# Attention ahead of a mixture of experts: input sets loaded in thirds, weight conversion moved to later steps with four word buffers

## The chip, the cores and the metric

One core of a Trainium2 chip runs the whole program. The metric is the device time of one execution in microseconds (us), taken as the median over runs. The engines are named as the profile names them: PE is TensorE's matmul, PEld its weight load, DVE is VectorE, ACT is ScalarE, POOL is GpSimd and SP is SyncE, which here issues transfers.

## The reference

Three layers follow each other. The first is attention with a sigmoid in place of the softmax, for 4 batches of 12 heads with 448 positions of 64 elements. Its output, laid out as 1792 tokens of 768, goes through a gate that gives each of 8 experts 224 tokens, and then through a feed-forward layer.

```python
scores = scale * np.matmul(q, k.transpose(0, 1, 3, 2)) - np.log(S)
attn = 1.0 / (1.0 + np.exp(-scores))
x = np.matmul(attn, v)
...
logits = x @ w_gate
...
h = np.maximum(x[mask] @ w1[e], 0.0)
out[mask] = h @ w2[e]
...
h = x @ w_in
g = np.maximum(h, 0.0) + alpha * np.minimum(h, 0.0)
return g @ w_out
```

The last layer's weights w_in and w_out arrive as 64-bit floating-point numbers, two 32-bit words each.

## The kernel before, in words

**The attention stage.** The heads are taken in 12 sets of four (three sets a batch). A set's q, k and v lie side by side in one tile `qkv` of 128 partitions, 1344 KB: q in its first third, k in its second, v in its last. The pool that holds it has three buffers. A set takes seven steps (`STEPS_OF`, L338): three for its first pair of heads, one for what is left of both pairs, three for the second pair. So there are 84 steps, numbered i. In each, `scores(i)` makes eight matmuls (L350) and one sigmoid on ACT (L353), and two steps later `values` makes eight matmuls with the result (L373). At the end of a pair ACT copies an accumulator out (L377, L381) and DVE adds the other (L379, L382).

**What is put between the steps.** After each batch, `turns` transposes the batch's output and stores its rows to DRAM (L315 on PE, L318 on ACT, L320 on SP), one of four turns a step, from the third step of the next batch's first set. Then `after_batch` computes the gate and compares the tokens' gate values with those of all tokens before them (L197 and L199 on DVE, L206 on PE), a little in every step and more in the later batches.

**The conversion of the last layer's weights.** `narrow` (L386) is a generator that turns the 64-bit words of w_in (16 parts) and of the first 13 blocks of w_out into 32-bit floating-point numbers, 29 parts in all. A part is fetched into a `words` tile by a transfer that POOL issues (L398, L400). ACT takes the absolute value of the upper words (L405, every second part; DVE does the others, L419) into `ct` and scales the lower words into `cl` (L427). DVE clamps, shifts and joins (L423, L425, L429), POOL adds `ct` and `cl` (L440), and the parts of w_out are stored to DRAM by a transfer of POOL's (L410). When part i has been added, the fetch of part i + 3 is issued, since there are three `words` buffers. The generator stops after each piece of its work, 102 times in all; `aside(i)`, called twice in each step, adds PACE to an account and takes one piece for each whole unit.

**The order of the work** is that of the program: each engine, and each engine's queue of transfers, takes its instructions in the order in which the Python code writes them, and waits only for data and for free buffers. A transfer that stands at some step of the code is thus issued as soon as its engine gets there. The main loop (L496 on) writes, for each step: scores, loads of later sets, `aside`, values, one piece of the work after a batch, `aside`.

**The loads.** Set 0 is loaded in five pieces before the loop: q and k of its first pair, v, q and k of its second pair (L105 to L109, all on SP). Set 1 is loaded in one transfer by ACT's queue after the first step's scores. Set n + 2 is loaded in one transfer on SP at the fourth step of set n, into the buffer of set n - 1.

```python
            if i == 0:
                load(1, eng=nc.scalar)
            n, at_step = divmod(i, len(STEPS_OF))
            if at_step == LATE + 1 and n + 2 < B * NQ:
                load(n + 2)
        aside(i)
```

Of the kernel before, what the change touches and what calls it, by code (L numbers as in the profile page):

```python
# [24 lines left out]
def attention_experts_ffn(  # L25
# [11 lines left out]
    nc = tc.nc  # L37
    B, NQ, P = qkv.shape[:3]
    N, DM = out.shape
# [38 lines left out]
    cv = att.enter_context(tc.tile_pool(name="cv", bufs=3))  # L78
# [7 lines left out]
    QV = 2 * S  # L86
    KC = S // P
    qkv_sb = {}

    def load(n, a=0, z=3 * QV, eng=nc.sync):  # L90
        if a == 0:
            qkv_sb[n] = ld.tile([P, 3 * QV], F32, name="qkv")
        eng.dma_start(qkv_sb[n][:, a:z], qkv[n // NQ, n % NQ, :, a:z])

    def q_of(n, r):
        return qkv_sb[n][:, r * S:(r + 1) * S]
# [4 lines left out]
    def v_of(n, c, h):  # L101
        o = 2 * QV + (c * 4 + h) * D
        return qkv_sb[n][:, o:o + D]

    load(0, 0, S)  # L105
    load(0, QV, QV + S)
    load(0, 2 * QV, 3 * QV)
    load(0, S, QV)
    load(0, QV + S, 2 * QV)  # L109

    warm = const.tile([1, 1], F32, name="warm")
    nc.vector.memset(warm, 0.0)
# [190 lines left out]
    def turns(b):  # L303


        x = xT[b]

        def turn(t0):
            w = min(P, S - t0)
            xt = aw.tile([P, DM], F32, name="xt", bufs=3)  # L310
            p = ps_s.tile([P, 2, 512], F32, name="psc")
            for i in range(HP):
                for s in range(w // D):
                    for z in range(2):
                        nc.tensor.matmul(p[halves[s], z, i * D:(i + 1) * D],  # L315
                                             x[halves[z], i, t0 + s * D:t0 + (s + 1) * D],
                                             ident[halves[z], halves[z]], start=True, stop=True)
            nc.scalar.copy(xt[:w].rearrange("p (i z d) -> p z i d", z=2, d=D),  # L318
                           p[:w, :, :HP * D].rearrange("p z (i d) -> p z i d", d=D))
            nc.sync.dma_start(x_dram[b * S + t0:b * S + t0 + w, :], xt[:w])  # L320

        return [lambda t0=t0: turn(t0) for t0 in range(0, S, P)]
# [7 lines left out]
    def keep_warm(ps, tag, n):  # L330
        p = ps.tile([P, 512], F32, name=tag)[:, :3 * P]
        for _ in range(n):
            nc.tensor.matmul(p, idle[:, :P], idle, start=True, stop=True)
# [6 lines left out]
    LATE = 2  # L340
    halves = [slice(0, D), slice(D, P)]

    def scores(i):
        n, r, c = steps[i]
        p = ps_s.tile([P, 2, 512], F32, name="psc")
        for s in range(2):
            for z in range(2):
                a = c * P + z * D if r is not None else KC * P
                w = r if r is not None else z
                nc.tensor.matmul(p[halves[z], s, :S], k_of(n, w, a, a + D)[halves[s]], q_of(n, w)[halves[s]],  # L350
                                 start=True, stop=True)
        AT[i] = aw.tile([P, 2, S], F32, name="at", bufs=LATE + 2)
        nc.scalar.activation(AT[i], p[:, :, :S], AF.Sigmoid, bias=bias, scale=1.0 / math.sqrt(D))  # L353

    def values(i):
        n, r, c = steps[i]
        b, m = divmod(n, NQ)
        if (r, c) == (0, 0):
            if m == 0:
                xT[b] = aw.tile([P, HP, S], F32, name="xT")  # L360
            PV[0, 1] = ps_v.tile([P, 512], F32, name="pav")
            PV[0, 0] = ps_v.tile([P, 512], F32, name="pav")
        if r is None:
            PV[1, 1] = ps_v.tile([P, 512], F32, name="pav")
        if (r, c) == (1, 0):
            PV[1, 0] = ps_v.tile([P, 512], F32, name="pav")
        a = AT.pop(i)
        for z in range(2):
            w = r if r is not None else z
            first = (w, z) == (1, 1) and r is None or (w, z) != (1, 1) and c == 0  # L370
            last = (w, z) == (0, 0) and r is None or (w, z) != (0, 0) and c == KC - 1
            for s in range(2):
                nc.tensor.matmul(PV[w, z][halves[s], :S], v_of(n, c, 2 * w + s if r is not None else s)[halves[z]],  # L373
                                 a[halves[z], s, :], start=first, stop=last)
        x = xT[b]
        if (r, c) == (0, KC - 1):
            nc.scalar.copy(x[:, 2 * m, :], PV[0, 1][:, :S])  # L377
        elif r is None:
            nc.vector.tensor_tensor(x[:, 2 * m, :], x[:, 2 * m, :], PV[0, 0][:, :S], op=OP.add)  # L379
        elif (r, c) == (1, KC - 1):  # L380
            nc.scalar.copy(x[:, 2 * m + 1, :], PV[1, 1][:, :S])  # L381
            nc.vector.tensor_tensor(x[:, 2 * m + 1, :], x[:, 2 * m + 1, :], PV[1, 0][:, :S], op=OP.add)  # L382
# [87 lines left out]
    FA = 13  # L470
    if wide:
        back = narrow([(True, f, 0) for f in range(NF)] + [(False, f, 0) for f in range(FA)],
                      cv, DM, ("words", 3), ("ct", 4), ("cl", 3))
    else:
        back = iter(())
        for f in range(NF):
            nc.gpsimd.dma_start(w_in_sb[:, :, f * P:(f + 1) * P], w_in[f].rearrange("p (c f) -> p c f", f=P))
# [3 lines left out]

    def aside(i):

        if i > 2:
            owed[0] += PACE
            while owed[0] >= 1:
                next(back, None)
                owed[0] -= 1

    nc.sync.dma_start(wg[:, :, :E], w_gate.rearrange("(c p) e -> p c e", p=P))  # L490
    nc.sync.dma_start(al, alpha.rearrange("(c p) -> p c", p=P))
    PACE = 0.64
    keep_warm(ps_m, "pm", 14)
    NS = len(steps)
    BS = NQ * len(STEPS_OF)
    for i in range(NS + LATE):  # L496
        if i < NS:
            scores(i)
            if i == 0:
                load(1, eng=nc.scalar)  # L500
            n, at_step = divmod(i, len(STEPS_OF))
            if at_step == LATE + 1 and n + 2 < B * NQ:
                load(n + 2)
        aside(i)
        k = i - LATE
        if k == NS - 1:
            final = after_batch(B - 1)
            final.pop(0)()
        if k >= 0:
            values(k)  # L510
        for turns_left in (rows_todo, todo):
            if turns_left:
                turns_left.pop(0)()
                break
        aside(i)
        if k >= 0 and k % BS == BS - 1:
            b = k // BS
            todo += after_batch(b) if b + 1 < B else final
            (rows_todo if b + 2 < B else rows_end).extend(turns(b))
# [777 lines left out]
```

## Time and profile before

| | |
|---|---|
| median of 3 runs | 1025.6 us (1024.71 to 1025.71) |
| the profiled execution | 1016.1 us |
| its span, first to last instruction | 1014.3 us |
| mean granted clock of TensorE | 0.977 |
| busy in the span: PE, DVE, ACT, POOL | 965.7, 659.2, 524.4, 223.0 us |
| attention stage | from 5.9 to about 187 us of the span |

The profiled execution is a single one and was 9.5 us shorter than the median of the timed runs. Times in the rows are microseconds from the start of its span. Busy time counts an engine's instructions, not its waits. In a row of a timeline, the bracket at the end gives the idle time of the engine ahead of the instruction and what ended it. A granted clock of 1.00 is the full clock of TensorE, 2.4 GHz, and 0.50 is half of it.

### The profile page before, as it was taken

How to read it: one execution, taken by the hardware profiler on the slowest of the kernel's cores; microseconds unless marked ns; L12 is line 12 of the kernel's file. 1: busy time of each engine (PE TensorE's matmuls, PEld its weight loads, DVE VectorE, ACT ScalarE, POOL GpSimd, SP SyncE). 2: the span in 40 equal slices, each digit the busy share in tenths (PEclk: the TensorE clock that was granted, in tenths of full speed). 3: DMA queues.
4: the chain of work that ended last, by engine and by line, in shares of the span. 5: the costliest groups of instructions: out<-in, count | busy, mean ns of one | idle time of the engine just before them, and what ended most of it. 6: DMA issues, size and time to landing. Idle time of an engine off the chain costs nothing.

```text
span 1014.3 us, 17190 instructions
## 1 busy us (share of the span) xinstructions
PE 965.7 (95%) x6729; PEld 792.4 (78%) x6729; DVE 659.2 (65%) x1258; ACT 524.4 (52%) x875; POOL 223.0 (22%) x300
## 2 busy tenths in 40 slices
PE   6999989869899999999999999999999999999995
PEld 2444433568898888899988899999899999999994
DVE  1868769797777685477777645876543477744342
ACT  3987867511364334366643344675443466644441
POOL 1545354221750001711000060300120111000001
PEclk8999999969899999999999999999999999999998
DMA  7776794465661220357303131871231157311211
GB/s 258 262 289 237 274 323 165 177 215 158 191 190 40 63 95 32 84 178 256 125 32 109 47 113 39 272 232 35 94 91 61 45 181 254 119 47 47 63 32 55
DMA packets 38643, 141.44 MB, mean 139 GB/s; under 512 B 8931, under 2 KB 9523, under 8 KB 37155
## 3 DMA queue, kind: packets, MB, share of 16 engines
q1 hardware_dynamic: 23186, 71.02, 21.7%
q0 software_dynamic: 15232, 67.95, 20.3%
q8 instruction: 53, 0.87, 0.4%
q10 hardware_dynamic: 144, 1.38, 0.3%
q14 instruction: 28, 0.22, 0.1%
HBM read 122.86 MB, written 17.46 MB: 138 GB/s over the span
## 4 chain that ended last, share of the span: by engine, by line
PE 74%; DVE 9%; ACT 7%; DMA 5%; issue 3%; POOL 2%; SPq 0%; DVEq 0%; ACTq 0%; POOLq 0%
PE pa L1129 20%; PE pz L1109 19%; PE pa L1027 15%; PE psc L350 4%; PE pav L373 4%; ACT si L963 2%; PE pa L912 2%; PE pa L932 2%; DMA qkv<-in_qkv_dram 1%; PE pa L1109 1%; PE pc L206 1%; DVE t L1030 1%; DVE g L199 1%; PE psc L315 1%; POOL pk L740 1%
## 5 line engine op out<-in xcount | busy, mean ns | idle before, releaser
L1129 PE MATMUL pa<-gx,so 128*128 128x448 f32 x1152 | 252.4, 369 | 0.4 <-DVE so L1074 0.3
L1109 PE MATMUL pz<-y,si 128*128 128x448 f32 x1080 | 231.0, 367 | 1.2 <-ACT R L182 1.2
L1129 PEld LDWEIGHTS pa<-gx,so 128*128 128x128 f32 x1152 | 213.9, 188 | 21.2 <-issue 2.5
L1109 PEld LDWEIGHTS pz<-y,si 128*128 128x128 f32 x1080 | 202.0, 188 | 19.3 <-ACT R L182 1.7
L1112 ACT ACTIVATE gx<-pz 128x448 f32<-128x448 f32 x60 | 32.7, 546 | 250.1 <-PE pz L1109 250.1
L1114 DVE SCALAR_TENSOR_TENSOR gx<-gx,nalpha 128x448 f32<-128x448 f32 x64 | 43.8, 684 | 151.9 <-ACT gx L1113 151.8
L1067 POOL DMA_DIRECT2D wo<-wo_dram x64 | 35.7, 559 | 438.9 <-DVE so L1074 253.8
L1027 PE MATMUL pa<-y,si 128*128 128x448 f32 x336 | 111.9, 386 | 1.2 <-DVE y L990 1.2
L1027 PE MATMUL pa<-gx,si 128*128 128x448 f32 x336 | 107.8, 378 | 0.0
L350 PE MATMUL psc<-qkv 64*64 64x448 f32 x672 | 98.2, 565 | 8.4 <-DMA qkv<-in_qkv_dram 6.8
L373 PE MATMUL pav<-at,qkv 64*64 64x448 f32 x672 | 99.8, 552 | 5.9 <-ACT xT L381 5.1
L353 ACT ACTIVATE at<-psc,bias 128x896 f32<-128x896 f32 x84 | 84.2, 1009 | 40.8 <-PE psc L350 40.5
L968 DVE TENSOR_TENSOR so<-wm,si 128x768 fp32r<-128x768 f32 (+1 forms) x98 | 103.9, 1064 | 2.1 <-PE pa L1129 1.1
L963 ACT CAST si<-wm 128x768 fp32r<-128x768 f32 (+1 forms) x98 | 89.7, 920 | 0.9 <-DMA wm<-in_w_dram 0.9
L1027 PE MATMUL pa<-gx,so 128*128 128x224 f32 x336 | 83.1, 268 | 0.5
L1027 PE MATMUL pa<-y,so 128*128 128x224 f32 x336 | 81.9, 271 | 1.6 <-DVE so L968 1.6
L373 PEld LDWEIGHTS pav<-at,qkv 64*64 64x64 f32 x672 | 33.6, 137 | 46.5 <-issue 32.6
L1027 PEld LDWEIGHTS pa<-y,so 128*128 128x128 f32 x336 | 65.4, 195 | 4.9 <-DVE so L968 2.2
L1030 DVE TENSOR_TENSOR t<-pa,t 128x224 f32<-128x224 f32 x98 | 38.3, 391 | 45.4 <-ACT t L1029 45.2
L1027 PEld LDWEIGHTS pa<-y,si 128*128 128x128 f32 x336 | 62.5, 193 | 5.1 <-ACT si L963 1.4
L1027 PEld LDWEIGHTS pa<-gx,so 128*128 128x128 f32 x336 | 63.9, 190 | 3.2 <-DVE so L968 2.2
L1118 DVE TENSOR_TENSOR gx<-gx 128x448 fp32r<-128x448 f32 x64 | 40.1, 626 | 40.5 <-ACT gx L1117 40.5
(209 smaller groups left out, 1445.5 us busy)
## 6 DMA issues: line engine op xcount, KB each, us to landing
wm<-in_w_dram SPq DMA_DIRECT2D x64, 384.0 KB, 3.6
wm<-in_w_dram SPq DMA_DIRECT2D x48, 512.0 KB, 4.5
wo<-wo_dram POOLq DMA_DIRECT2D x64, 384.0 KB, 3.4
qkv<-in_qkv_dram SPq DMA_DIRECT2D x10, 1344.0 KB, 8.4
words<-in_w_in_dram POOLq DMA_DIRECT2D x16, 768.0 KB, 5.5
words<-in_w_out_dram POOLq DMA_DIRECT2D x13, 768.0 KB, 5.9
wo_dram<-ct POOLq DMA_DIRECT2D x13, 384.0 KB, 3.5
x_dram<-xt SPq DMA_DIRECT2D x12, 384.0 KB, 4.2
```

Of the source, the lines that this page charges most:

```text
L350: nc.tensor.matmul(p[halves[z], s, :S], k_of(n, w, a, a + D)[halves[s]], q_of(n, w)[halves[s]], start=True, stop=True)
L353: nc.scalar.activation(AT[i], p[:, :, :S], AF.Sigmoid, bias=bias, scale=1.0 / math.sqrt(D))
L373: nc.tensor.matmul(PV[w, z][halves[s], :S], v_of(n, c, 2 * w + s if r is not None else s)[halves[z]], a[halves[z], s, :], start=first, sto ...
L963: nc.scalar.copy(hi, w)
L968: nc.vector.tensor_tensor(lo, w, hi.bitcast(F32), op=OP.subtract)
L1027: nc.tensor.matmul(o, a[:, c, :], y, start=(c == 0 and s == 0), stop=(c == k - 1 and s == 1))
L1030: nc.vector.tensor_tensor(t, p[:, :CAP], t, op=OP.add)
L1067: nc.gpsimd.dma_start(RW[f], wo_dram[f * P:(f + 1) * P, :])
L1109: nc.tensor.matmul(z[:, :n], a[:, c, :], m[:, c, :n], start=(c == 0 and s == 0), stop=(c == HP - 1 and s == 2))
L1114: nc.vector.scalar_tensor_tensor(t, dn, nalpha[:, f:f + 1], up, op0=OP.mult, op1=OP.add)
L1118: nc.vector.tensor_tensor(gl, t, gh.bitcast(F32), op=OP.subtract)
L1129: nc.tensor.matmul(acc[d][:, :n], a[:, d * P:(d + 1) * P], m, start=(f == 0 and s == 0), stop=(f == NF - 1 and s == 2))
```

## The change

There are four edits.

- `load` uses SP alone, and set 1 is loaded right behind set 0's pieces, in one transfer, where it was issued by ACT after the first step's scores.
- Set n + 2 is loaded in three transfers, q, k and v, at steps 3, 4 and 5 of set n, where it was one transfer at step 3.
- The conversion has four `words` buffers and two `cl` buffers, where it had three of each. The fetch issued after part i is thus that of part i + 4.
- `aside` begins at step 9 and no longer at step 3, and its pace is 0.68 of a piece a call, where it was 0.64.

```diff
--- before.py
+++ after.py
@@ -87,10 +87,10 @@
     KC = S // P
     qkv_sb = {}
 
-    def load(n, a=0, z=3 * QV, eng=nc.sync):
+    def load(n, a=0, z=3 * QV):
         if a == 0:
             qkv_sb[n] = ld.tile([P, 3 * QV], F32, name="qkv")
-        eng.dma_start(qkv_sb[n][:, a:z], qkv[n // NQ, n % NQ, :, a:z])
+        nc.sync.dma_start(qkv_sb[n][:, a:z], qkv[n // NQ, n % NQ, :, a:z])
 
     def q_of(n, r):
         return qkv_sb[n][:, r * S:(r + 1) * S]
@@ -107,6 +107,7 @@
     load(0, 2 * QV, 3 * QV)
     load(0, S, QV)
     load(0, QV + S, 2 * QV)
+    load(1)
 
     warm = const.tile([1, 1], F32, name="warm")
     nc.vector.memset(warm, 0.0)
@@ -470,7 +471,7 @@
     FA = 13
     if wide:
         back = narrow([(True, f, 0) for f in range(NF)] + [(False, f, 0) for f in range(FA)],
-                      cv, DM, ("words", 3), ("ct", 4), ("cl", 3))
+                      cv, DM, ("words", 4), ("ct", 4), ("cl", 2))
     else:
         back = iter(())
         for f in range(NF):
@@ -481,7 +482,7 @@
 
     def aside(i):
 
-        if i > 2:
+        if i > 8:
             owed[0] += PACE
             while owed[0] >= 1:
                 next(back, None)
@@ -489,18 +490,18 @@
 
     nc.sync.dma_start(wg[:, :, :E], w_gate.rearrange("(c p) e -> p c e", p=P))
     nc.sync.dma_start(al, alpha.rearrange("(c p) -> p c", p=P))
-    PACE = 0.64
+    PACE = 0.68
     keep_warm(ps_m, "pm", 14)
     NS = len(steps)
     BS = NQ * len(STEPS_OF)
     for i in range(NS + LATE):
         if i < NS:
             scores(i)
-            if i == 0:
-                load(1, eng=nc.scalar)
             n, at_step = divmod(i, len(STEPS_OF))
-            if at_step == LATE + 1 and n + 2 < B * NQ:
-                load(n + 2)
+
+            if LATE < at_step <= LATE + 3 and n + 2 < B * NQ:
+                a = (at_step - LATE - 1) * QV
+                load(n + 2, a, a + QV)
         aside(i)
         k = i - LATE
         if k == NS - 1:
```

## Rows read from the trace of the kernel before

**Rows 1.** The page's 40 slices of the span (25.4 us each), tenths

```profile
PE   6999989869899999999999999999999999999995
PEclk8999999969899999999999999999999999999998
```

**Rows 2.** Windows, 24 to 187 us: length; PE, PEld, DVE, ACT, POOL busy; PEclk

```profile
24.00:187.00 163.00, 153.52 (x1905) 66.62 (x1900) 129.47 (x190) 128.78 (x158) 78.82 (x68) 0.98 0.70 247
```

**Rows 3.** The chain of waits, 1 to 32 us: start, us, what

```profile
2.62 15.05 DMA qkv<-in_qkv_dram
```

**Rows 4.** DMA issues, 2 to 6 us: KB of each, median us to landing

```profile
qkv<-in_qkv_dram SPq DMA_DIRECT2D x2, 224.0 KB, 15.0
```

**Rows 5.** Timeline of PE: start, us, instructions [idle before, releaser]

```profile
17.81 1.02 PE L350 MATMUL psc<-qkv 64*64 64x448 f32 x3 [6.76 <-DMA qkv<-in_qkv_dram]
...
96.12 0.59 PE L373 MATMUL pav<-at,qkv 64*64 64x448 f32 x2 [1.52 <-ACT xT L381]
...
143.42 0.97 PE L373 MATMUL pav<-at,qkv 64*64 64x448 f32 x4 [2.58 <-ACT xT L381]
```

**Rows 6.** DMA queues, 6 to 18 us: packets, MB, share of 16 engines

```profile
DMA packets 3645, 3.95 MB, mean 329 GB/s; under 512 B 2929, under 2 KB 3160, under 8 KB 3517
...
q0 software_dynamic: 378, 2.03, 41.8%
q10 hardware_dynamic: 144, 1.38, 27.1%
```

**Rows 7.** Windows, two stretches after a stop of PE

```profile
17.80:22.30 4.50, 4.49 (x25) 1.72 (x29) 0.00 (x0) 1.01 (x1) 0.00 (x0) 0.51 0.88 307
...
97.00:101.00 4.00, 4.00 (x74) 2.06 (x73) 3.90 (x5) 2.60 (x3) 2.52 (x2) 0.57 0.87 310
```

**Rows 8.** Timeline of ACT and of POOL around two late words

```profile
93.84 0.92 ACT L405 ACTIVATE ct<-words 128x768 f32<-128x768 f32 x1 [1.32 <-DMA words<-in_w_in_dram]
...
141.16 0.90 ACT L405 ACTIVATE ct<-words 128x768 f32<-128x768 f32 x1 [2.10 <-DMA words<-in_w_out_dram]
...
128.89 0.60 POOL L400 DMA_DIRECT2D words<-in_w_out_dram  x1
...
133.87 0.59 POOL L400 DMA_DIRECT2D words<-in_w_out_dram  x1
```

**Rows 9.** Timeline of PE, POOL and SP at the start

```profile
5.88 1.73 PE L350 MATMUL psc<-qkv 64*64 64x448 f32 x16
...
9.33 0.98 PE L373 MATMUL pav<-at,qkv 64*64 64x448 f32 x8 [0.36 <-DMA qkv<-in_qkv_dram]
...
1.80 1.83 POOL L398 DMA_DIRECT2D words<-in_w_in_dram  x3
...
4.64 12.97 SPq L93 DMA_DIRECT2D qkv<-in_qkv_dram  x1
```

**Rows 10.** Timeline of ACT at step 9 and of DVE at the stage's end

```profile
30.76 1.02 ACT L353 ACTIVATE at<-psc,bias 128x896 f32<-128x896 f32 x1
...
187.11 0.62 DVE L382 TENSOR_TENSOR xT<-xT,pav 128x448 f32<-128x448 f32 x1 [2.07 <-ACT xT L381]
```

**Rows 11.** The tile qkv: DMA issues (ns, first and last start), landing times

```profile
L93 SPq DMA_DIRECT2D qkv<-in_qkv_dram x15: 327/370/12970, 0.8 to 139.4; - x15
...
DMA to landing us min/median/max: 2.6/8.0/18.4
```

**Rows 12.** Waits of SP's queue, 0 to 187 us: total, times, longest

```profile
SPq L93 <- PE pav L373: 71.6, 7, 12.8
```

**Rows 13.** Timeline of POOL (add 26) and of ACT (Copy 28)

```profile
176.16 2.04 POOL L440 TENSOR_TENSOR ct<-ct,cl 128x768 int32<-128x768 int32 x1 [2.17 <-ACT at L353]
...
180.72 0.94 ACT L427 ACTIVATE cl<-words 128x768 int32<-128x768 uint32 x1
```

**Rows 14.** Windows, instructions on ct (DVE, ACT, POOL), then on cl (ACT, POOL)

```profile
23.00:187.00 164.00, 88.62 (x101) 13.98 (x15) 63.63 (x42) 0.98 0.69 245
...
23.00:187.00 164.00, 26.94 (x29) 55.70 (x29) 0.98 0.69 245
```

## The prediction

> **What bounds the kernel now.** I read the page's slices first. TensorE is at nine tenths or more almost everywhere; the slices that are not full, and those where its clock is low, lie in the first quarter, which is the attention stage [rows 1]. The whole change lies in that stage, so I read only it. A window over 24 to 187 us shows that no engine is full there: TensorE 153.5 of 163.0 us, VectorE 129.5, ScalarE 128.8, POOL 78.8 [rows 2]. The stage is a chain that goes round between PE, ACT and DVE, and a stop of one of them soon stops PE. Behind the stage follow routing and the experts, whose start hangs on its end; I let a gain here reach the end of the program in full.
>
> Next I looked for the stops of PE. There are three that a transfer causes.
> - The start. The chain of waits has one transfer of 15.05 us, from 2.62 us [rows 3]: the last two pieces of set 0 (q and k of the second pair) took 15.0 us to land [rows 4], and step 3's scores, which need them, went on only at 17.81, after 6.76 us in which PE was idle [rows 5]. From 6 to 18 us POOL's words (2.03 MB) and ACT's load of set 1 (1.38 MB) were moved beside what was left of set 0 on SP's queue [rows 6]. From 17.8 to 22.3 us PE ran at a granted 0.51, the lower of its two levels, 1.2 GHz [rows 7].
> - ACT's Abs of words at 93.84 waited 1.32 us for its transfer, and PE then stood idle 1.52 us; ACT's Abs at 141.16 waited 2.10 us, and PE stood idle 2.58 us [rows 5, 8]. After each, the granted clock was 0.57 over four microseconds, 97 to 101 [rows 7] and 145 to 149 alike.
>
> **The change part by part.**
> *Set 1 from SP at once.* The load leaves ACT's queue and stands on SP's behind set 0's five pieces. What competes with the last two pieces is then the words alone. Lower bound of the landing: together these pieces have the 448 KB of the piece before them (set 0's v), which PE could use at 9.33 us, 3.45 us after the first pair (5.88) [rows 9]; at that rate they are there at 9.33 + 3.45 = 12.8. Upper bound: 17.8, nothing gained. Between them: the window moved 3.95 MB in 12 us, 0.33 MB a us, so without ACT's 1.38 MB [rows 6] they land some 4 us sooner. I take 14.0, a gain of 3.8 us; words' fourth transfer is the reason not to take the lower end. PE's idle time shrinks from 6.8 to about 3 us, but the stops of 1.5 and 2.6 us below also brought the low clock [rows 5, 7], so I leave in one such stretch: 0.43 missing of 4 us is 1.7 us lost. Before, 0.49 missing of 4.5 us lost 2.2: 0.5 us gained (bounds 0 and 2.2). Set 1 itself follows on the same queue: 1.38 MB at 0.33 MB a us is 4.2 us, 18.2 or, beside the words, 20 us. Step 7 comes four steps after step 3, which from 17.81 to step 9's sigmoid at 30.76 took 2.2 us each [rows 5, 10]: at 22. The tiny gate and alpha loads stand behind it; nobody needs them before step 23. SP stood 12.97 us in the issue of set 2 behind them, from 4.64 [rows 9], and the longest landing, 18.4 us [rows 11], is set 2's, at 23; with 4.2 us of set 1 ahead of it, it is there at some 28, and step 14 comes five steps after step 9, not before 33. No cost.
>
> The Trainium skill speaks against this gain: "DMA: Bandwidth & Descriptors", section "Issuing engines are not separate DMA queues", says that transfers started by any engine run on the same 16 engines and interleave, and that another issuer saves only issue time. By it alone the sum would have 0 for the first wait. The same page's "Queues, rings and completion order" has each engine take turns between the queues' rings, by which SP gets every second turn and not every third. I go by [rows 4, 6].
>
> *Thirds at steps 3, 4, 5.* Twenty more issues on SP, at 0.37 us in the median [rows 11], 7.4 us; SP waits 71.6 us for PE to release a set [rows 12], so they are hidden. Nothing on SP waits for a step: where no row store stands between, the three thirds are issued one after the other as soon as the buffer is free, so the spreading is mostly in the packets. After each batch's end the thirds stand behind row stores, and the last is up to two steps later. Set n+2 is needed eleven steps after step 3, some 22 us, nine after step 5, some 18; the median landing is 8.0 us [rows 11]. Cost 0; without that cover a late set would stop PE as the words do, 3 to 4 us a time.
>
> *Four word buffers.* At the start POOL's program has nothing ahead of the first fetches that waits, so they go out at 1.80 us whatever step they stand at [rows 9]: now four. Later every fetch goes out one part earlier. The fetch that came late at 141.16 left at 133.87, and would leave where the one before it left, at 128.89 [rows 8]: 5.0 us for a wait of 2.10. The one at 93.84 was later by less, and gains a part's length too. The two stops cost 1.52 + 2.58 us idle and 0.43 x 4 = 1.7 us each at the low clock [rows 5, 7]: 7.5 us together. VectorE and ScalarE get time back in such a stop, so I take 6.0 (bounds 0 and 7.5). POOL's one more issue at the start, 1.83 us for three [rows 9], 0.6, falls before it has anything to convert.
>
> *Two "cl" buffers.* ScalarE's Copy of part i must now wait for POOL's add of part i-2, not i-3. Nearest in time are the last parts: Copy 28 starts at 180.72, add 26 ended at 176.16 + 2.04 = 178.20, 2.5 us before [rows 13]. Cost 0 at this margin; it is the rival below.
>
> *Begin at i > 8, pace 0.68.* (That is six steps later, not five.) The 102 yields took 80 steps at 1.28, and take 75 at 1.36, to step 83 and not 82. About 6 x 1.28 = 7.7 yields move from steps 3 to 8 into the rest. VectorE's operations of the conversion sum to 88.6 us, 0.87 a yield, ScalarE's two to 14.0 + 26.9 = 40.9, 0.40 a yield [rows 14]: 6.7 and 3.1 us move. Bounds 6.7 (VectorE full), 0 (hidden wholly) and, below nothing, -3.1, ScalarE's work gone from steps 3 to 8. Its share was 129.5 of 163.0 [rows 2], so I take 0.79 x 6.7 = 5.3. At the end the last VectorE operation comes a step later, into 2.07 us that VectorE waits before 187.11 [rows 10]: 0.
>
> *Sum:* -3.8 - 0.5 - 6.0 + 5.3 = -5.0 us. The profiled execution took 1016.1 us (its span 1014.3) and would take 1011.1; the median of the timed runs is 1025.6, 9.5 above it, and I take the same difference off that: **1020.6 us**. 0.2%, 2.05 us, is about what a measurement of this kernel can tell from none: 1023.5 to 1027.7 is "same".
>
> **The rivals.**
> - *The denser conversion is hidden.* For it: 20% of VectorE's and ScalarE's time is free [rows 2]. Then -10.3 us: 1015.3.
> - *The first wait stays:* the same transfers share the same engines, and words' fourth takes the place of set 1's beside the last pieces. Against: words' packets were beside all of set 0 already, and ACT's came on top. Without the 4.3 us: 1024.9. The rule on issuing engines in the Trainium skill's "DMA: Bandwidth & Descriptors", above, would have it so.
> - *The words come late again,* because the transfers and not the buffers are short: the denser pace asks 6% more. For it: the late one took 141.16 - 133.87 = 7.3 us from issue to use [rows 8], more than a part's 5.4 (29 parts in the 156 us from 30.76 to 187.11 [rows 10]). Against: the two late ones miss by 2.1 us or less and leave 5 us earlier. -4.3 + 5.3 = +1.0: 1026.6.
> - *Slower: ScalarE waits for POOL.* In the third and fourth batch VectorE carries the comparisons too, falls behind, POOL's add follows it, and the Copy with two buffers holds ScalarE, its sigmoids and PE. It decides once add i-2 ends later than Copy i's place, 2.5 us beyond what [rows 13] show, at two places or more. Each costs like the two stops, (1.52 + 2.58) / 2 + 1.7 = 3.75. With VectorE full: -4.3 - 6.0 + 6.7 + 2 x 3.75 = +3.9: 1029.5.
> - *It does not do what it says:* the first fetches and most thirds do not move with their steps. That is in the sum already.
>
> **How the numbers follow.** Forecast 0.48, hidden conversion 0.17, first wait 0.10, words late again 0.11, slower 0.14. The second goes to faster with the forecast: 0.65. The third and fourth are same: 0.21. Slower 0.14. The forecast's own range is 1016.0 to 1023.5. The range for eight in ten takes in the centres of the hidden conversion, the first wait and the late words, and leaves out the slower rival and the tail below: 1014.0 to 1027.0.
>
> **What would show it.** Step 3's scores should go on at about 14 us and not 17.8, and step 9's sigmoid come at 26 and not 30.76 [rows 10]; ScalarE's Abs should wait for no words, and the low clock at 97 and 145 should be gone; the stage should end near 182 where it ended at 187. VectorE's share over the stage should rise. Wrong: a ScalarE Copy with a wait for POOL's add; PE waiting for qkv beyond step 3; a words wait above 1 us; new stretches at 0.5 after 30 us.

## The result, and the profile after

The changed kernel took 1011.48 us (1009.40 to 1013.34, four runs), the kernel before beside it 1025.65 us (1024.71 to 1031.52, four runs): a ratio of 0.9849 [0.9805, 0.9894]. That is faster, as forecast, but the forecast was 1020.6 us and its range ended at 1014.0. The profiled executions are closer: 1009.74 us after (span 1007.7) against 1016.1 before (span 1014.3), 6.4 us less, where the sum of the steps was 5.0. The kernel before has short executions (1011 to 1022 us) and long ones (1023 to 1033 us), in a mix that changes with the occasion: its recorded runs were long, its profiled execution was short, and the ratios below leave out runs over 1.5% above a kernel's fastest.

The page after; its slices answer to [rows 1]. The first slice, with PE's first stop, has gone from 6 to 7 and its clock from 8 to 9, and the sixth, with the second late word, from 8 to 9. The eighth and ninth differ because the stage's end and the routing behind it lie there, some 8 us sooner.

```profile
PE   7999999789899999999999999999999999999994
PEclk9999999879999999999999999999999999999998
```

PE's timeline after. Step 3's scores [rows 5] go on at 14.21 and not 17.81. The second line is a stop that the kernel before did not have at this place; the three later profiles of the changed kernel have it too, 2.35, 2.52 and 2.49 us.

```profile
14.21 1.01 PE L351 MATMUL psc<-qkv 64*64 64x448 f32 x3 [2.91 <-DMA qkv<-in_qkv_dram]
...
146.52 0.35 PE L207 MATMUL pm<-g,OH 112*32 112x448 bf16 x1 [2.38 <-DVE g L200]
```

DVE's timeline after: what PE waited for at 146.52, three comparisons that took 2.82 us where the next one took 0.44, and the last addition of the stage, at 178.68 where [rows 10] have 187.11. The last line is from POOL's timeline: the conversion's addition ran from 144.22 to 146.22, and of the three comparisons it is the first, which began beside it, that took 2.00 us; the other two took 0.54 and 0.44.

```profile
144.47 2.82 DVE L200 TENSOR_SCALAR g<-R,M 112x448 bf16<-112x448 f32 x3
...
147.67 0.44 DVE L200 TENSOR_SCALAR g<-R,M 112x448 bf16<-112x448 f32 x1
...
178.68 0.62 DVE L383 TENSOR_TENSOR xT<-xT,pav 128x448 f32<-128x448 f32 x1 [2.07 <-ACT xT L382]
...
144.22 2.00 POOL L441 TENSOR_TENSOR ct<-ct,cl 128x768 int32<-128x768 int32 x1 [2.98 <-issue]
```

Three windows after. The start's stretch at the low clock is shorter (0.65 over 4.5 us, in [rows 7] 0.51), the one at 97 us is gone, and behind the new stop PE ran at 0.55, near the lower of its two levels, 1.2 GHz.

```profile
14.10:18.60 4.50, 4.39 (x32) 1.80 (x36) 0.00 (x0) 1.33 (x2) 0.00 (x0) 0.65 1.03 324
97.00:101.00 4.00, 3.95 (x60) 1.94 (x64) 2.92 (x4) 3.96 (x6) 1.45 (x3) 1.00 1.01 351
147.20:150.70 3.50, 3.50 (x22) 0.77 (x18) 3.07 (x7) 2.09 (x3) 0.93 (x2) 0.55 0.83 297
```

The DMA queues after, 6 to 18 us, against [rows 6]: ACT's queue with its 1.38 MB is gone from the window, and SP's queue has 1.92 MB. The small packets are not ACT's: they are those of the gate and alpha loads on SP's queue, and half of them now come after 18 us, since set 1 stands ahead of them.

```profile
DMA packets 2278, 4.70 MB, mean 392 GB/s; under 512 B 1431, under 2 KB 1666, under 8 KB 2151
...
q0 software_dynamic: 512, 2.78, 57.1%
q1 hardware_dynamic: 1766, 1.92, 45.2%
```

The waits of ACT after, 24 to 180 us, all five rows that the view has: none is for words, where [rows 8] showed two, and none is for POOL's addition. ACT's sigmoid of step 9 stands at 25.79 us in the timeline; [rows 10] had 30.76.

```profile
ACT at L354 <- PE psc L351: 22.8, 31, 3.3
ACT xT L382 <- PE pav L374: 2.8, 1, 2.8
ACT xt L319 <- PE psc L316: 2.0, 3, 0.9
ACT xt L319 <- DMA x_dram<-xt: 1.0, 1, 1.0
ACT ct L406 <- DMA wo_dram<-ct: 0.3, 1, 0.3
```

At the start POOL now issues four fetches and SP all six loads without a pause (the timelines of POOL and of SP, against [rows 9]).

```profile
1.80 2.35 POOL L399 DMA_DIRECT2D words<-in_w_in_dram  x4
```

```profile
0.77 2.77 SPq L93 DMA_DIRECT2D qkv<-in_qkv_dram  x6
```

### The profile page after: what moved, and what is told of

Its sections match the earlier page's. It is cut to its first block, busy times and chain, and to the rows that moved or that the text cites. A ratio compares the mean times of both kernels' runs of the same rounds, so it can differ in the third digit from the quotient of the medians.

```text
span 1007.7 us, 17223 instructions
## 1 busy us (share of the span) xinstructions
PE 963.7 (96%) x6729; PEld 789.4 (78%) x6729; DVE 660.2 (66%) x1258; ACT 524.4 (52%) x875; POOL 222.2 (22%) x300
## 4 chain that ended last, share of the span: by engine, by line
PE 69%; DVE 10%; ACT 6%; DMA 5%; POOL 4%; issue 4%; SPq 0%; DVEq 0%; POOLq 0%; ACTq 0%
PE pa L1130 20%; PE pz L1110 19%; PE pa L1028 11%; PE psc L351 4%; PE pav L374 4%; POOL pk L741 3%; DMA wm<-in_w_dram 3%; PE pa L913 2%; ACT si L964 2%; PE pa L1110 1%; PE pc L207 1%; DMA qkv<-in_qkv_dram 1%; DVE t L1031 1%; PE pa L1169 1%; ACT t L1030 1%
## 5 line engine op out<-in xcount | busy, mean ns | idle before, releaser
L1028 PE MATMUL pa<-y,si 128*128 128x448 f32 x336 | 109.8, 379 | 1.3 <-DVE y L991 1.1
```

Source lines behind the costliest of these rows:

```text
L1028: nc.tensor.matmul(o, a[:, c, :], y, start=(c == 0 and s == 0), stop=(c == k - 1 and s == 1))
```

## The experiments

In each series the kernel before ran beside the others, and ratios are to it, with their 95% interval. Microseconds gained or lost are worked out from the ratio; the two medians alone can differ from it by 0.1%. Medians of the kernel before in the five series: 1016.4, 1015.7, 1015.2, 1027.0, 1023.5 us, and 1015.3 beside the last run.

**The kernel before again, unchanged**

> The kernel before, unchanged, to see its spread and a second profile. The profiled execution took 1016.1 us and the timed runs 1024.7 to 1031.5; the change gained 6.4 us between the two profiled executions (1016.1 to 1009.74) and 14.2 between the medians. Theory A: executions of the kernel before differ by how often a transfer of words comes too late; then a slower execution has more than the two Abs waits and more than the two low-clock stretches (97 and 145 us) of the first profile, and its ACT waits for words sum to more than 4.0 us. Rival B: the executions differ behind the attention stage; then the stage ends near 187 us again and the difference stands later in the span.

Measured: 1015.38 us, 0.999 [0.9967, 1.0012]. None of the 33 runs of the kernel before beside it lay outside 1012.6 to 1020.1. So the 1025.65 of the recorded result is not what this kernel always takes, and the profiled 1016.1 is no oddity. The stage's end varies as well: it stands at 182.76 in this run's profile, where the first profile had 187.11, and ACT's waits for words sum to 3.2 us, where they were 4.0.

**Each part alone, on the kernel before.** Set 1's load, at once and on SP's queue:

```diff
     load(0, QV + S, 2 * QV)
+    load(1)
...
-                load(1, eng=nc.scalar)
+                pass
```

> Only set 1's load moved to SP behind set 0's pieces. Theory A (the start is worth what it showed): step 3's scores go on at about 13 to 14.2 us and not 17.8, the low clock after it lasts one stretch and not two, and the time falls by 3 to 5 us, to about 1021. Rival B (what is gained at the start is lost again, because the conversion then runs at the same steps beside faster ones and the late words stay): no change beyond 0.2%.

Measured: 1013.64 us, 0.9963 [0.9944, 0.9983], 3.7 us less. PE's timeline in this run has step 3's scores at 14.44. In all twelve profiles with set 1 on SP they go on at 13.7 to 14.9, and in seven of the eight with set 1 on ACT's queue at 17.5 to 18.1 (in the eighth, a later one of the four buffers alone, at 15.32):

```profile
14.44 1.01 PE L351 MATMUL psc<-qkv 64*64 64x448 f32 x3 [3.37 <-DMA qkv<-in_qkv_dram]
```

The buffers of the conversion:

```diff
-                      cv, DM, ("words", 3), ("ct", 4), ("cl", 3))
+                      cv, DM, ("words", 4), ("ct", 4), ("cl", 2))
```

> Only four words buffers and two cl buffers. Theory A (the late words are the main cost): no Abs waits for words, no low clock at 97 and 145 us, and the time falls by 6 to 10 us, to 1016 to 1020. Rival B (the transfers themselves are short, so another buffer only moves the wait): waits for words remain, and the time stays within 2 us of 1025.6. The start: a fourth transfer of words stands beside set 0's last pieces, so step 3's scores go on at 17.8 or up to 2 us later.

Measured: 1011.5 us, 0.9951 [0.993, 0.9971], 5.0 us less. ACT waits for no words in it, and for no addition of POOL. PE's start is as before.

The later begin and the denser pace:

```diff
-        if i > 2:
+        if i > 8:
...
-    PACE = 0.64
+    PACE = 0.68
```

> Only the later begin (i > 8) and the pace 0.68. Theory A of the prediction (VectorE and ScalarE carry 7.7 more pieces in steps 9 to 83, at their share): slower by about 5 us, 1031. Rival B (the denser pieces go into time in which both wait anyway, and steps 3 to 8 run free): within 2 us. Rival C (with three words buffers a denser pace makes more transfers late): slower by 3 to 4 us for each further late one, with waits for words above 4.0 us in sum.

Measured: 1020.3 us, 1.0042 [1.0025, 1.006], 4.3 us more. On three buffers the words now come later still: 7.0 us of waits in the view of ACT's waits, where the kernel before had 4.0.

```profile
ACT ct L405 <- DMA words<-in_w_out_dram: 3.8, 2, 3.4
ACT ct L405 <- DMA words<-in_w_in_dram: 3.2, 1, 3.2
```

Then, in the second series, the thirds alone:

```diff
-            if at_step == LATE + 1 and n + 2 < B * NQ:
-                load(n + 2)
+            if LATE < at_step <= LATE + 3 and n + 2 < B * NQ:
+                a = (at_step - LATE - 1) * QV
+                load(n + 2, a, a + QV)
```

> Only the loads of sets 2 to 11 in thirds at steps 3, 4 and 5. Theory A of the prediction (hidden, nothing gained): within 2 us of the kernel before. Rival B (smaller packets of the sets let the words through sooner): the waits for words fall under 2 us in sum and the time falls by 2 to 4 us. Rival C (sets late): waits of PE for qkv behind step 3 and a time above by 2 us or more.

Measured: 1016.87 us, 1.0012 [0.999, 1.0035]: no difference shown, though the waits for words were 1.8 us in its profile and not 3.2 or 4.0.

**The changed kernel again, and with one part undone.**

> The changed kernel, unchanged, beside the kernel before on the same chip. The kernel before gave 1016.4 us in the median of 33 runs in the last series, where the first four runs gave 1024.7 to 1031.5, so the ratio 0.9849 compares runs taken apart. Theory A (the gain is that of the profiles, 6 to 7 us): ratio 0.993 to 0.995, time near 1009 to 1011. Rival B (the change is worth 14 us whatever the series): ratio 0.985, time near 1002.

Measured: 1012.1 us (1009.3 to 1014.2, twelve runs), 0.9973 [0.9956, 0.9991]; the kernel before took 1015.69 (1011.6 to 1021.8, 32 runs). The changed kernel is where it was in the recorded result, and the kernel before is 10 us lower. On such an occasion the change is worth some 3 us. The four parts alone come to -3.7 - 5.0 + 4.3 + 1.2 = -3.2, each with an interval of some 2 us to either side.

Whole loads in place of thirds (the last diff, reversed):

> The changed kernel with sets 2 to 11 loaded whole at step 3 again. Theory A (thirds are worth nothing): as the changed kernel, within 2 us. Rival B: 2 to 4 us slower than the changed kernel, with waits for words back.

Measured: 1011.0 us, 0.9958 [0.9938, 0.9978], against 0.9973 with thirds: the intervals overlap, and the thirds are worth nothing that shows.

Begin and pace as they were (`i > 2`, 0.64):

> The changed kernel with the conversion begun at i > 2 and the pace 0.64 again. Alone, the later begin cost 0.42% (4.3 us). Theory A (parts add up): 4 us faster than the changed kernel, ratio to the kernel before about 0.989. Rival B (the later begin costs only by late words, which four buffers take away): as the changed kernel, within 2 us. Rival C (the later begin is needed beside the earlier set 1, since it leaves the transfers to sets 1 and 2): slower than the changed kernel by 2 us or more, with waits for words or qkv in the first 40 us.

Measured: 1009.06 us, 0.9938 [0.9917, 0.9958], 3 us under the changed kernel in the same series. So this part costs some 3 us in the changed kernel too, where words are never late. Which half of it, the third series asked, with the early begin and the dense pace together:

```diff
-        if i > 8:
+        if i > 2:
```

> The changed kernel with the conversion begun at i > 2, as before, but at the pace 0.68, so that it ends some six steps earlier, near step 77. It parts the later begin from the denser pace. Theory A (the cost of 3 to 4 us is that of the last steps, in which the conversion of the changed kernel still runs beside the comparisons of the third batch): as the kernel with i > 2 and 0.64 or faster, ratio 0.991 to 0.994, the stage's end at 178 us or before. Rival B (the cost is the density itself, at every step): as the changed kernel, 0.996 to 0.998.

Measured: 1011.12 us, 0.9963 [0.9948, 0.9977], nearer to the changed kernel (0.9973) than to the run before this one (0.9938). That points to the density as the cost and not to the late begin, but the runs are of two series and the intervals of 0.9963 and 0.9938 overlap. The profiles do not show where the 3 us lie: the stage's last addition stands at 179.37 us here, at 178.68 to 179.02 in the changed kernel's four, and at 178.32 with the old begin and pace, in a profile of that run's slowest execution (1011.32 us).

The three buffers put back into the changed kernel:

```diff
-                      cv, DM, ("words", 4), ("ct", 4), ("cl", 2))
+                      cv, DM, ("words", 3), ("ct", 4), ("cl", 3))
```

> The changed kernel with three words and three cl buffers again. Theory A (parts add up): 5 us slower than the changed kernel, ratio about 1.002. Rival B (a denser pace with three buffers makes more words late, as the later begin alone did, 7.0 us of Abs waits): 7 us or more slower than the changed kernel, ratio 1.004 or above, with Abs waits for words above 6 us in sum.

Measured: 1018.55 us, 1.0021 [0.9999, 1.0042]. By the parts alone it should be -3.7 + 4.3 + 1.2 = +1.8, and it is +2.1 (0.0021 of 1015.2). The words' waits are back in the view of ACT's waits:

```profile
ACT ct L406 <- DMA words<-in_w_out_dram: 3.5, 2, 2.1
...
ACT ct L406 <- DMA words<-in_w_in_dram: 2.3, 1, 2.3
```

**The two parts that gain, without the other two.** The diffs of set 1 and of the buffers together, on the kernel before:

> The kernel before with set 1 on SP at once and four words and two cl buffers, without the thirds and with the conversion at i > 2 and pace 0.64 as before: the two parts that gained alone. Theory A (parts add up): -3.8 - 5.0 = -8.8 us, ratio 0.991, and 2 to 3 us faster than the changed kernel without its later begin (0.9938), the thirds being the difference. Rival B (both gain by the same slack, late words and the low clock): no more than the 0.9938 of that kernel.

Measured: 1006.96 us (1006.1 to 1009.1), 0.9925 [0.9904, 0.9945]. This is the best of the kernels here, 4 to 5 us below the changed one, which stood in other series. Its stage ends first as well (DVE's timeline):

```profile
176.06 0.62 DVE L383 TENSOR_TENSOR xT<-xT,pav 128x448 f32<-128x448 f32 x1 [2.07 <-ACT xT L382]
```

If a denser pace costs, a sparser one might gain more: this kernel with `i > 0` and a pace of 0.61.

> The best kernel so far (set 1 on SP at once, four words and two cl buffers; 0.9925) with the conversion spread thinner still: begun at i > 0 with pace 0.61, so that its 102 pieces end at step 84 as nearly as they can. Theory A (the density of the conversion is what costs, 0.25 to 0.42% for 0.68 against 0.64): 1 to 3 us faster than 0.9925, ratio 0.990 to 0.9915. Rival B (0.64 is thin enough, or the pieces that then lie in the last steps delay the stage's end): 0.9925 or above.

Measured: 1016.02 us (1009.0 to 1019.6, twelve runs), 0.9927 [0.9884, 0.9969], in the fourth series, in which the kernel before took 1027.02. Its stage ends at 176.10, no earlier. Nothing here shows it faster than 0.64, and a ratio to a kernel before of two kinds is too coarse to tell.

**The long executions.** The changed kernel beside it in that fourth series:

> The changed kernel once more beside the kernel before. Theory A (the gain is a few microseconds: parts of -3.8, -5.0, +4.3 and +1.2 us): ratio between 0.993 and 0.998, and the kernel before near 1015 to 1016 us. Rival B (the 0.9849 of the first runs is the change's own): ratio 0.985, and the kernel before near 1025.

Measured: 1012.04 us (1009.1 to 1015.3, six runs), 0.9887 [0.9828, 0.9946]. Of the kernel before, 14 of 17 runs took 1023 to 1032 us and three 1012 to 1016. So the large lead is back: the kernel before is longer, and the changed kernel is where it was. The fifth series took it apart:

> The kernel before once more, for a profile of a long execution. On two occasions it gave 1025 to 1032 us (first four runs; 14 of 17 in the last series), on three others 1011 to 1022, while the changed kernel gave 1009 to 1015 on all. Theory A (on some chips its transfers land later, and the three words buffers then give out more often): a long execution, should the profile show one, has Abs waits for words well above the 3.2 to 4.0 us of the two profiles so far, and more low-clock stretches before 190 us. Rival B (the long executions lose their time elsewhere): the stage ends at 183 to 188 us as before and the time is lost behind it.

> Set 1 on SP at once, alone, once more. On a chip where the kernel before takes 1016 us: -3.8 us again, ratio 0.996. On one where it takes 1027: Theory A (late words decide there) still long executions, at most 5 us gained; Rival B (the start decides there): 1012 to 1015.

> Four words and two cl buffers, alone, once more. On a chip where the kernel before takes 1016 us: -5.0 us again, ratio 0.995. On one where it takes 1027: Theory A (late words decide there): 1011 to 1016, 11 us or more gained; Rival B: no more than 5 us gained.

> The loads in thirds, alone, once more. On a chip where the kernel before takes 1016 us: within 2 us again. On one where it takes 1027: Theory A (the sets' large packets hold up the words there, and thirds let them through): some of the long executions go, 3 us or more gained; Rival B: as the kernel before.

Measured: the kernel before 1028.73 us (four runs), set 1 alone 1023.47 (1009.5 to 1029.1), the buffers alone 1020.46 (five of twelve runs at 1009.7 to 1013.5, seven at 1019.6 to 1026.8), the thirds alone 1027.51 (1017.6 to 1034.3); ratios to the kernel before in the series 1.0109 [1.0044, 1.0175], 1.0007 [0.996, 1.0054], 0.9952 [0.9898, 1.0007] and 1.0053 [1.0008, 1.0097]. The first of these is the same kernel against itself and not 1, since 14 of the 29 runs beside it were short (1012.8 to 1018.5); no ratio of this series is finer than that. No part alone is rid of the long executions. The chip does not decide, as the expectations supposed: each of two chips gave both kinds on different occasions. Some of these profiles are of long executions, and one can be laid beside a short one of the same kernel. First the end of the stage and the first feed-forward matmul in the long one (1028.87 us; timelines of DVE and of PE), then the same in the short one (1013.14 us):

```profile
185.97 0.62 DVE L382 TENSOR_TENSOR xT<-xT,pav 128x448 f32<-128x448 f32 x1 [2.07 <-ACT xT L381]
...
317.92 3.81 PE L1109 MATMUL pz<-y,si 128*128 128x448 f32 x18
```

```profile
182.76 0.62 DVE L382 TENSOR_TENSOR xT<-xT,pav 128x448 f32<-128x448 f32 x1 [2.07 <-ACT xT L381]
...
301.09 3.81 PE L1109 MATMUL pz<-y,si 128*128 128x448 f32 x18
```

The stage ends 3.2 us later, the feed-forward begins 16.8 us later: 13.6 of these 16.8 us are lost behind the attention stage, in code that the change does not touch. Late words are not what makes this execution long: ACT's waits for them sum to 4.4 us in it and to 3.2 in the short one. Nor is a late end of the stage: 187.11 and 190.21 are found in profiles of 1016.1 and 1022.12 us (the kernel before, the pace alone), which do not have the stops below. ACT's timeline of the long one shows where: its copies of the first expert's products stand for 3.68 and 7.98 us, and the profile knows no engine or transfer of this core that released them ("remote").

```profile
273.40 0.35 ACT L1029 COPY t<-pa 128x224 f32<-128x224 f32 x1 [0.54 <-PE pa L1027]
...
279.00 0.35 ACT L1029 COPY t<-pa 128x224 f32<-128x224 f32 x1 [3.68 <-remote]
...
288.89 0.35 ACT L1029 COPY t<-pa 128x224 f32<-128x224 f32 x1 [7.98 <-remote]
```

In the short one the same copies follow each other every 1.9 us without a wait of that kind:

```profile
274.34 0.35 ACT L1029 COPY t<-pa 128x224 f32<-128x224 f32 x1
...
276.22 0.35 ACT L1029 COPY t<-pa 128x224 f32<-128x224 f32 x1
...
278.11 0.35 ACT L1029 COPY t<-pa 128x224 f32<-128x224 f32 x1
```

Two windows of the long one, then of the short one: PE, DVE and ACT all stand, POOL goes on with its 16 scatters (2.55 us of 3.00), and the transfers nearly cease (the last two numbers, share and GB/s), because nothing frees the buffers for the experts' weights (SP's queue waits 9.4 us in one piece for VectorE there). The third number from the end is the granted clock, 0.50 in the long one, the lower level, after PE had stood.

```profile
283.00:286.00 3.00, 0.23 (x1) 0.00 (x0) 0.00 (x0) 0.00 (x0) 2.55 (x5) 0.50 0.19 63
286.00:289.00 3.00, 0.00 (x0) 0.00 (x0) 0.00 (x0) 0.11 (x1) 1.58 (x3) 0.50 0.01 1
```

```profile
283.00:286.00 3.00, 3.00 (x20) 2.72 (x20) 2.00 (x4) 1.86 (x4) 2.63 (x3) 1.00 0.91 267
286.00:289.00 3.00, 3.00 (x21) 2.87 (x20) 2.31 (x4) 2.17 (x5) 1.48 (x3) 1.00 0.42 145
```

The profile of the thirds alone (1034.33 us) has the same two stops, and that of set 1 alone (1019.94 us) one of 4.53 us. None of the other 17 profiles of this study, 1006.2 to 1022.1 us, those of the kernel before among them, has a stop of ACT over 3 us on that line behind the first product. ACT's timeline with the thirds alone:

```profile
281.73 0.34 ACT L1030 COPY t<-pa 128x224 f32<-128x224 f32 x1 [3.64 <-remote]
291.65 0.34 ACT L1030 COPY t<-pa 128x224 f32<-128x224 f32 x1 [8.00 <-remote]
```

The last run was the changed kernel once more:

> The changed kernel once more, beside the kernel before. In the profiles of three long executions (of the kernel before at 1028.9 us, of the thirds alone at 1034.3, of the first step's loads alone at 1019.9) ScalarE stands for 3.7 and 8.0 us (4.5 us in the last) at the first wide products of the first expert behind the attention stage (line 1029 of the kernel before), waiting for TensorE, while GpSimd issues its 16 scatters; in none of the profiles of shorter executions does it. Theory A: the changed kernel does not run into this stop, whatever the occasion. Then its runs lie between 1008 and 1016 us, also where the runs of the kernel before reach 1023 to 1032 us, its median is near 1011.5, and no wait of ScalarE on that line is over 3 us beyond the first. Theory B: it runs into it as the four-buffers kernel did (half of its runs at 1019.6 to 1026.8 us), and the earlier series only missed it. Then some runs lie 10 to 16 us above the others, at 1020 to 1028 us, and the lead over the kernel before is the 3 to 4 us of the quiet occasions. If the kernel before shows no run over 1023 us, the run does not tell them apart.

Measured: 1010.61 us (1008.3 to 1016.2, eleven runs), 0.996 [0.9938, 0.9981], but the kernel before showed no run above 1021.9, so the run decides nothing between the two theories; as to the lead on such an occasion it agrees with the series before, some 3 to 4 us.

## Why the prediction was right or wrong

**The step that failed** is the last of the sum: "the median of the timed runs is 1025.6, 9.5 above it, and I take the same difference off that". It took the 9.5 us for a constant between profiled and timed runs. They are the distance from a short execution of the kernel before to its long ones. In the one long execution of it that was profiled most of such a distance, 13.6 us, lies behind the stage, where ScalarE's two stops are; the recorded runs have no profile, so that theirs lies there too is likely and not shown. By their times, 1009 to 1015 us, the changed kernel's four recorded runs were not long, nor the six beside the fourth series. The sum against the profiled execution alone gave 1011.1; the profile came out at 1009.74 and the median at 1011.48. That this is so close is in part luck: short executions of the kernel before spread over 1011 to 1022 us, and the second profile of it took 1013.14. The distance should have been a bound of the range, 0 to 9.5, with 1011.1 at its lower end.

**The start** was right: step 3's scores at 14.21 (forecast 14.0), and set 1 alone gives 3.7 us where the sum had 3.8 + 0.5. Step 9's sigmoid came at 25.79 (26), but not by the start alone: with set 1 alone it stands at 27.57, and the later begin alone, whose steps 3 to 8 are free of the conversion, has it at 29.76 instead of 30.76. The Trainium skill's "DMA: Bandwidth & Descriptors", section "Issuing engines are not separate DMA queues", has another issuer save only issue time. By the prediction's reading of it the first wait would have stayed as it was; the run with set 1 alone ended it 3.4 us sooner (14.44 against 17.81). The measurement decides: here it counted whether the 1.38 MB ran beside the awaited pieces or stood behind them on their queue. The rival of the first wait falls.

**The four word buffers** were right in place and somewhat high in size: no wait for words is left, and the part alone measures 5.0 us (forecast 6.0, bounds 0 and 7.5). The rival that words come late again, and the slower one, ScalarE waiting for POOL's addition, do not appear in the waits of any profile with these buffers; the margin on "cl" sufficed at the dense pace too.

**Begin and pace** was right in sign and close in size (+4.3 alone, some +3 in the changed kernel; forecast +5.3), and the rival that the denser conversion is hidden falls: undoing it gained 3 us, undoing the begin alone nothing that shows. VectorE's share did rise, from 0.794 to 0.845 (130.1 of 154 us, 24 to 178). Its mechanism was right only in part and is not fully shown. Alone, it works at least partly through later words (waits of 7.0 us). In the changed kernel's profile the one stop of PE over 1 us behind the start is VectorE's, at 146.52, and PE fell to 0.55 behind it; it comes from a comparison that began beside POOL's addition. But the kernel before has such a stop as well (1.15 us at 127.76), and so has the changed kernel with the old begin and pace (1.40 us at 123.39), so this stop alone does not account for the 3 us. My forecast of no new stretch at the low clock beyond 30 us did not hold, by this one.

**The thirds** were right: nothing either way (1.0012 with them alone, 0.9958 without them against 0.9973 with them).

**The whole.** The stage ended 8.4 us sooner (178.68 against 187.11; forecast near 182), and 6.6 us of it reached the end of the span. Against the second profile of the kernel before it is 4.1 us (182.76), which is closer to the repeated lead. Repeated on occasions when the kernel before takes 1015 to 1016, the lead is 0.9973 [0.9956, 0.9991] and 0.996 [0.9938, 0.9981], 3 to 4 us: the 5.0 of the sum is on the high side there, and the 14 us of the recorded result are these and the distance to the long executions of the kernel before, which the changed kernel did not have on those occasions.

**What stays open** is why the changed kernel was not long in the ten runs that stood beside long ones, and so the cause of some 10 of the 14 us. Neither set 1 nor the buffers nor the thirds alone does it; set 1 and the buffers together were not run beside long executions at the old pace (with the sparse pace they gave 1009.0 to 1019.6). Nor is it shown what holds ACT's copies: TensorE's matmuls that they wait for have ended in the trace, and POOL's scatters run through the stop, but in the short execution they run beside the same products without one.

## What to carry to other kernels

Before a sum is set against a median, see whether the profiled execution lies among the timed ones; where it lies 1% below, the difference may be a mechanism of its own, to be bounded and not carried over. A transfer that an early step waits for is helped by taking off its queues what is not needed yet, and a late word by one more buffer, both for nothing here; filler work between a chain's steps is not free in the gaps of busy engines: a 6% denser pace cost 3 to 4 us with VectorE and ScalarE below 85% busy, while a thinner one than before gained nothing that shows. Of a change with several parts, run those that gain without the others: here they beat the whole by 4 to 5 us.

## What the runs showed that was not expected

- One program took some 1013 or 1029 us on one core, and most of the 13.6 us that a long execution lost behind the attention stage lay in one place, at the first expert's products: two stops of ScalarE, 3.7 and 8.0 us, at the same two places in two different kernels.
- POOL's scatters took 0.94 us each during that stop, and up to 1.99 us each in the short execution, where the other engines and the weights' transfers ran on beside them.
- Three comparisons on VectorE took 2.82 us, where the next one took 0.44 (the timeline after, above). The first of the three began while POOL's addition ran, and that is the pattern of all 20 profiles: between 20 and 190 us a comparison that began while an addition of the conversion ran on POOL took 1.84 us in the median (81 of them), any other 0.45 (799). The conversion's own TENSOR_SCALAR operations on VectorE do the same (1.98 against 0.56 us on `ct`, 1.81 against 0.55 from `words`), while VectorE's sum of an accumulator (`xT<-xT,pav`, 0.62 us) does not change.
